# SwiGLU written with tanh, eight PSUM banks assigned by the schedule, and attention spread over the FFN chunks

## The chip, the cores and the metric

The kernel runs on one core of one Trainium2 chip. The metric is the device time of one execution in microseconds (us). A run is called slow where it lies more than 1.5 per cent above the fastest of the same kernel; such runs are left out of every ratio.

In the profile, PE is the tensor engine, PEld its weight loads, DVE the vector engine, ACT the scalar engine, POOL the GpSimd engine, and SP the engine that issues many of the DMAs. All operations are issued through helpers, so a group of instructions is told by its tiles (`psc`, `Hs`), not by its line. A letter at the end of a tile's name is its place in a ring of buffers. The granted clock is the share of its full clock that PE was given; the DMA share adds up packet times over the 16 DMA engines, so it can pass 1.

## The reference

Two stages follow one another: causal attention with a decay bias over 8 batches of 8 heads, 576 positions and head size 64, and then RMS norm and a SwiGLU feed-forward network (FFN) over the resulting 4608 tokens.

```python
scores = scale * np.matmul(q, k.transpose(0, 1, 3, 2))
bias = -(cum[:, :, :, None] - cum[:, :, None, :])      # cum: running sum of max(s, 0)
scores = np.where(causal, -1000000000.0, scores + np.minimum(bias, 0.0))
attn = softmax(scores)                                  # (shortened)
x = np.matmul(attn, v)  # then heads side by side: (4608, 512)   (shortened)
xn = x / rms * rms_g
g = xn @ w_gate                                         # d_ff = 1536
silu = g * (1.0 / (1.0 + np.exp(-g)))
return (silu * (xn @ w_val) @ w_out)
```

## The kernel before

The kernel records its operations in a `Plan`. Each has a duration from a table and a key. A list scheduler then walks through simulated time, takes at each step the ready operation with the lowest key, and so fixes one order for each engine. The chip runs these orders with semaphores; if an operation in the order is late, everything behind it on that engine waits.

The FFN works in nine chunks of 512 tokens. Chunk c needs the attention of the tokens up to 512(c+1), and a batch has 576 tokens, so the attention of batch c+1 runs beside chunk c, and the last two chunks have no attention beside them (the ninth batch doesn't exist). FFN1 is the gate and value products with the gating, FFN2 is the output product.

PSUM is used as four pairs of banks: pairs 0 and 1 serve the scores, pairs 0 to 2 the FFN1 groups, the two halves of pair 2 the outputs in turn, and the two halves of pair 3 everything small.

```python
PS = [pp.tile([128, 2, DM], fp32, name=f"ps{chr(97 + i)}") for i in range(4)]
...  # cut
def small_bank():
    return nxt("small", [PS[3][:, 0, :], PS[3][:, 1, :]])
...  # cut: unit_scores, one pair of heads in one half of the queries
        mms(0.42, items, key=key)
        e = Es[u] = nxt("E", E)
        x = I("act", "activation", 0.93, key=key, kind="exp", out=e, in_=st, func=AF.Exp,
              scale=0.125)
        ...  # cut: causal masks on GpSimd (affine_select)
...  # cut
def ffn1_group(c, o, n, f0, key):
    P = nxt("pair", PS[0:3])
    ...  # cut: eight matmuls for the gate into P[:, 0], for the value into P[:, 1]
    sl = nxt("S", S_sb)
    silu = I("act", "activation", 0.51, key=key, kind="silu", out=sl, in_=P[:, 0, :],
             func=AF.Silu)
    I("dve", "tensor_tensor", 0.61, key=key, out=Hs[:, f0 : f0 + m, o : o + n],
      in0=sl.rearrange("p (i n) -> p i n", i=m),
      in1=P[:, 1, :].rearrange("p (i n) -> p i n", i=m), op=ALU.mult)
    return silu

def ffn2(c, key, step):
    t0 = c * DM
    for tb in range(4):
        O = nxt("O", [PS[2][:, 0, :], PS[2][:, 1, :]])
        ...  # cut: twelve matmuls into O
        o = nxt("osb", osb)
        I("dve", "tensor_copy", 0.61, key=key + step * (tb * FB + FB), out=o, in_=O)
        ...  # cut: o is stored
```

The exponentials and Silu have different tables in ACT. To keep table loads few, the main loop forbids FFN1 of a chunk before the exps of the attention before it, and the exps before all Silus of the chunk:

```python
for c in range(NCH):
    K = 100 * c
    ...  # cut
    new = [ffn1_group(c, o, n, f0, K + 50 * i / len(plan)) for i, (o, n, f0) in enumerate(plan)]
    for x in new:
        R.after(x, *exps)
    silus = new
    b = c + 1
    ...  # cut: preparation of batch b (K and Q transposed, V weighted), loads of batch b + 1
    ffn2(c, K + 50, 0.8)
    if b < B:
        exps = attention(b, K + 40, False)
        for x in exps:
            R.after(x, *silus)
```

So the scores and exps of attention can run beside FFN2 only, which is a third of a chunk's FFN matmuls.

Of the kernel before, what the change touches and what calls it, by code (L numbers as in the profile page):

```python
# [34 lines left out]

class Op:
    __slots__ = ("eng", "us", "lat", "fn", "key", "kind", "preds", "succ", "start", "done",
                 "n", "dma", "name", "wait")


class Plan:
# [4 lines left out]
    TABLE = 1.3  # L46

    def __init__(self):
        self.ops = []
        self.hist = {}  # L50
        self.key = 0.0
        self.last_kind = {}

    def add(self, eng, us, fn, outs, ins, key=None, lat=0.0, kind=None, dma=0.0, name=""):
# [3 lines left out]
        o.preds, o.n = {}, len(self.ops)  # L58
        for aps, write in ((ins, False), (outs, True)):
            for ap in aps:  # L60
                if ap is None or "DRAM" in str(ap.space):
                    continue
                h = self.hist.setdefault(ap.name, ([], []))
                m = _mask(ap)
                for w, wm in h[0]:
                    if wm & m and w is not o:
                        o.preds[w.n] = True
                if write:
                    for r, rm in h[1]:
                        if rm & m and r is not o:  # L70
                            o.preds.setdefault(r.n, False)
                    h[0][:] = [(w, wm & ~m) for w, wm in h[0] if wm & ~m]
                    h[1][:] = [(r, rm & ~m) for r, rm in h[1] if rm & ~m]
                    h[0].append((o, m))
                else:
                    h[1].append((o, m))
# [7 lines left out]
    def schedule(self):  # L84
# [12 lines left out]
        order = []  # L97

# [9 lines left out]

        for o in ops:
            if not left[o.n]:  # L110
                pool.setdefault(o.eng, []).append((ready(o), o))
        while any(pool.values()):
            best = None
            for e, cand in pool.items():
                if not cand:
                    continue
                f = free.get(e, 0.0)
                t = max(f, min(r for r, _ in cand))
                now = [(o.key, o.n, r, o) for r, o in cand if r <= t + 0.02]
                k = min(now, key=lambda x: x[:2])  # L120
# [13 lines left out]
            if o.dma:  # L134
                begin = max(self.dma_free, s + o.us + 1.2)
                self.dma_free = begin + o.dma
                o.done = self.dma_free + 1.4
            order.append(o)
            for q in o.succ:
                left[q.n] -= 1  # L140
                if not left[q.n]:
                    pool.setdefault(q.eng, []).append((ready(q), q))
# [10 lines left out]
def kernel(  # L153
# [35 lines left out]
    NE = 9  # L189
# [19 lines left out]
    ones = pers.tile([BH, S], fp32, name="ones")  # L209
# [3 lines left out]
    peak = pers.tile([128, B, HP], fp32, name="peak")  # L213
    nrm = pers.tile([128, B, 3], fp32, name="nrm")
    knrm = pers.tile([128, 1], fp32, name="knrm")
    mhalf = pers.tile([128, 3], fp32, name="mhalf")
    hones = pers.tile([128, 2], fp32, name="hones")
# [4 lines left out]
    spare = [xnT[0:KP, i, NTOK - H * KC * D : NTOK] for i in range(4)]  # L222
    k_raw, q_raw = (t.rearrange("p (h c d) -> p h c d", h=H, c=KC) for t in spare[0:2])
    k_pk, q_pk = (t.rearrange("p (c h d) -> p c h d", h=H, c=KC) for t in spare[2:4])
# [4 lines left out]
    gB = mp.tile([128, DM], fp32, name="gB")  # L229
# [13 lines left out]
    S_sb = ring(NS, [128, DM], bf16, "S_sb")  # L243
# [3 lines left out]
    PS = [pp.tile([128, 2, DM], fp32, name=f"ps{chr(97 + i)}") for i in range(4)]  # L247

    R = Plan()
# [3 lines left out]
    def I(eng, method, us, key=None, kind=None, dma=0.0, **kw):  # L253
        outs = [kw[n] for n in ("out", "accum_out") if n in kw]
        ins = [a for n, a in kw.items()
               if n not in ("out", "accum_out") and isinstance(a, bass.AP)]
        f = getattr(ENG[eng], method)
        return R.add(eng, us, lambda: f(**kw), outs, ins, key=key, lat=LAT[eng], kind=kind,  # L258
                     dma=dma, name=outs[0].name)
# [5 lines left out]
    def mms(us, items, key=None):  # L265
        def emit():
            for out, lhsT, rhs, st, sp, tr in items:
                if tr:
                    nc.tensor.matmul(out, lhsT=lhsT, rhs=rhs, is_transpose=True, start=st, stop=sp)  # L269
                else:  # L270
                    nc.tensor.matmul(out, lhsT=lhsT, rhs=rhs, start=st, stop=sp)  # L271
        return R.add("pe", us, emit, [i[0] for i in items],
                     [i[1] for i in items] + [i[2] for i in items], key=key, lat=0.22,
                     name=items[0][0].name)
# [7 lines left out]

    def small_bank():
        return nxt("small", [PS[3][:, 0, :], PS[3][:, 1, :]])

    def lay(bank, dt, pattern=None, n=None, **sizes):
        a = bank if dt == fp32 else bank.bitcast(dt)
# [4 lines left out]
    def load_runs(b, which, h0, h1, key):  # L292
        dst, src = ((k_raw, k), (q_raw, q))[which]
        return I("pool", "dma_start", 0.8, key=key, dma=3.95 * (h1 - h0) / 8,
                 out=dst[:, h0:h1, :, :].rearrange("p h c d -> p h (c d)"),
                 in_=src[b, h0:h1, :, :].rearrange("h (p c) d -> p h (c d)", c=KC))
# [22 lines left out]
    def prep_pack(which, h0, h1, key):  # L319
        src, dst = ((k_raw, k_pk), (q_raw, q_pk))[which]  # L320
        I("dve", "tensor_copy", 0.17 * (h1 - h0), key=key, out=dst[:, :, h0:h1, :],
          in_=src[:, h0:h1, :, :].rearrange("p h c d -> p c h d"))

    def prep_transpose(b, which, hp, key, eng):
        src, dst = ((k_pk, KT), (q_pk, QT))[which]
        t = lay(small_bank(), bf16, "p (c t) -> p c t", n=S, c=KC)
        mms(0.4, [(t[:, c, :], src[:, c, 2 * hp : 2 * hp + 2, :].rearrange("p h d -> p (h d)"),
                   ident_bf[0:KP, 0:KP], c == 0, c == KC - 1, True) for c in range(KC)], key=key)
# [4 lines left out]
        else:  # L333
            I("act", "activation", 0.56, key=key, out=o, in_=i, func=AF.Copy)

    def prep_cast(b, which, key):
        src, dst = ((k_nat, k_bf), (q_nat, q_bf))[which]
        out = (KT, QT)[which][b % 2]
        for sc in range(NB):
            n = 128 if sc < 4 else 64  # L340
            I("dve", "tensor_copy", 0.4, key=key, out=dst[0:n, sc], in_=src[0:n, sc])
            I("sp", "dma_start_transpose", 0.7, key=key, dma=0.8,
              out=out[:, :, sc * 128 : sc * 128 + n], in_=dst[0:n, sc])

    def prep_peak(b, hp, key):
        I("dve", "tensor_reduce", 0.68, key=key, out=peak[:, b, hp : hp + 1],
          in_=QT[b % 2][:, hp, :], axis=AX.X, op=ALU.max, apply_absolute_value=True)

    def prep_norm(b, i, key):
        if b < NRUN:  # L350
            n, src = KP, k_pk[:, 2 * i : 2 * i + 2, :, :].rearrange("p c h d -> p (c h d)")
        else:
            n = 128 if i < 2 else 64
            src = k_bf[0:n, 2 * i : min(2 * i + 2, NB), :].rearrange("p c m -> p (c m)")
        w = src.shape[1]
        I("act", "activation", 1.15 if w > DM else 0.74, key=key, out=sq_scr[0:n, 0:w], in_=src,
          func=AF.Square, accum_out=nrm[0:n, b, i : i + 1])
# [18 lines left out]
    def decay(key):  # L376
        I("dve", "tensor_scalar", 0.5, key=key, out=s_all, in0=s_all, scalar1=0.0, scalar2=None,
          op0=ALU.max)
        I("dve", "tensor_tensor_scan", 1.3, key=key, out=cum, data0=ones, data1=s_all, initial=0.0,
# [23 lines left out]
    def check_all(key):  # L403
        I("dve", "tensor_reduce", 0.1, key=key, out=knrm, in_=nrm, axis=AX.XY, op=ALU.max)
        kT = lay(small_bank(), fp32, n=128)[0:1, :]
        mms(0.2, [(kT, knrm, ident_F, True, True, True)], key=key)
        kmax = mp.tile([1, 1], fp32, name="kmax")
        I("dve", "tensor_reduce", 0.2, key=key, out=kmax, in_=kT, axis=AX.X, op=ALU.max)
        qq = mp.tile([128, B, HP], fp32, name="qq")
        I("dve", "tensor_tensor", 0.1, key=key, out=qq, in0=peak, in1=peak, op=ALU.mult)  # L410
        t = lay(small_bank(), fp32, n=2)[0 : BH // 2, :]
        mms(0.1, [(t, qq.rearrange("p b h -> p (b h)"), hones, True, True, False)], key=key)
        qn = mp.tile([BH // 2, 1], fp32, name="qn")
        I("dve", "tensor_reduce", 0.1, key=key, out=qn, in_=t, axis=AX.X, op=ALU.max)
        qT = lay(small_bank(), fp32, n=BH // 2)[0:1, :]
        mms(0.1, [(qT, qn, ident_F[0 : BH // 2, 0 : BH // 2], True, True, True)], key=key)
        ok = mp.tile([1, 4], fp32, name="ok")
        I("dve", "tensor_reduce", 0.1, key=key, out=ok[:, 0:1], in_=qT, axis=AX.X, op=ALU.max)
        I("dve", "tensor_tensor", 0.1, key=key, out=ok[:, 1:2], in0=ok[:, 0:1], in1=kmax,
          op=ALU.mult)  # L420
        I("dve", "tensor_scalar", 0.1, key=key, out=ok[:, 2:3], in0=ok[:, 1:2], scalar1=QK_MAX,
          scalar2=None, op0=ALU.is_le)
        t2 = lay(small_bank(), fp32, n=1)[0:1, :]
        mms(0.1, [(t2, ok1[:, 0:1], ones[:, 0:1], True, True, False)], key=key)
        I("dve", "tensor_tensor", 0.1, key=key, out=ok[:, 3:4], in0=ok[:, 2:3], in1=t2,
          op=ALU.mult)
        I("dve", "tensor_scalar", 0.1, key=key, out=flag, in0=ok[:, 3:4], scalar1=BH - 0.5,
# [6 lines left out]
    def unit_scores(b, u, key, Es, pair):  # L434
        hp, hf = u % HP, u // HP
        st = pair
        items = []
        gs = GROUPS[hf]
        for i, (kb, c0, q0, q1) in enumerate(gs):
            for j in range(2):  # L440
                rs = slice(j * 64, j * 64 + 64)
                items.append((st[:, j, c0 : c0 + q1 - q0],
# [4 lines left out]
        x = I("act", "activation", 0.93, key=key, kind="exp", out=e, in_=st, func=AF.Exp,  # L447
              scale=0.125)
# [3 lines left out]
        if hf == 1:  # L452
            last = e[:, :, 448:512]
            I("pool", "affine_select", 0.27, key=key, out=last, in_=last,
              pattern=[[0, 2], [1, 64]], compare_op=ALU.is_ge, fill=0.0, base=0,
              channel_multiplier=-1)
        return x

    def unit_av(b, u, key, Es):
# [10 lines left out]
        mms(0.04 + 0.06 * len(plan),  # L470
# [4 lines left out]
        I("dve", "reciprocal", 0.17, key=key, out=z, in_=AV[:, :, :, 64])  # L475
        I("dve", "tensor_tensor", 0.35 if hf == 0 else 0.48, key=key,
# [8 lines left out]
    def att_alpha(b, t0, t1, key):  # L485
        m, y = al[b % 2][:, 0, t0:t1], al[b % 2][:, 1, t0:t1]
        I("pool", "tensor_scalar", 0.17, key=key, out=m, in0=ss[b % 2][:, t0:t1],
          scalar1=1.0 / DM, scalar2=1e-6, op0=ALU.mult, op1=ALU.add)
        I("pool", "tensor_tensor", 0.8, key=key, out=y, in0=m, in1=mhalf[:, 0 : t1 - t0],
          op=ALU.pow)  # L490

    def att_scale(b, tb, key):
# [342 lines left out]
```

## Time and profile before

| | before |
|---|---|
| time, median of 3 runs | 430.75 us (430.5 to 431.23) |
| span of the profiled run, mean granted clock | 428.3 us, 0.989 |
| PE busy | 362.4 us, 85% |
| DVE, ACT, POOL busy | 257.2, 205.5, 179.5 us |
| ACT table loads | 16, 20.5 us |
| first FFN1 matmul | 38.6 us |
| end of FFN2 of chunks 0, 6, 8 | 91.2, 350.1, 422.3 us |

The page of the profile, first the busy time of each engine, then PE's busy share in 40 slices (tenths), then the chain of waits that ended last:

```profile
span 428.3 us, 7402 instructions
...
PE 362.4 (85%) x2808; PEld 214.6 (50%) x2843; DVE 257.2 (60%) x498; ACT 205.5 (48%) x327; POOL 179.5 (42%) x267
...
PE   0566978869988998899889988998899989979973
...
PE 76%; DVE 14%; ACT 4%; issue 3%; DMA 2%; POOL 0%; DVEq 0%; ACTq 0%; POOLq 0%
...
```

PE is both the busiest engine and three quarters of the chain. From the list of groups, the table loads (count, then busy us and mean ns of one, then the idle time ahead of them):

```profile
...
L258 ACT ACT_TABLE_LOAD x16 | 20.5, 1283 | 1.1 <-PEq L819 0.8
...
```

A table by stage gives the span of a stretch, then each engine's busy time (and instructions), the clock, the DMA share and GB/s. The four stretches are the start, chunk 0 (with 3.5 us after its end), chunk 4, and chunk 7, which has no new attention beside it:

```profile
...
core 0: us, PE busy (x) PEld busy (x) DVE busy (x) ACT busy (x) POOL busy (x), PEclk, DMA share, GB/s
0.00:38.60 38.60, 15.97 (x173) 11.87 (x174) 23.83 (x57) 16.67 (x27) 26.28 (x45) 1.00 1.07 182
38.60:94.70 56.10, 45.61 (x416) 32.56 (x420) 37.21 (x68) 30.86 (x50) 29.51 (x41) 0.97 0.81 150
224.50:266.40 41.90, 39.02 (x271) 18.63 (x275) 29.38 (x56) 24.10 (x41) 22.48 (x33) 1.00 0.75 134
350.10:386.70 36.60, 33.31 (x159) 15.17 (x160) 13.89 (x22) 8.49 (x14) 0.65 (x1) 1.00 0.08 29
...
```

A steady chunk such as 4 takes 41.9 us and has 39.0 us of PE work; chunk 7 takes 36.6 us with 33.3 us (the busy time of a pipelined matmul record overlaps its neighbours a little; start to start the 144 FFN steps of a chunk take 31.1 us).

Where chunk 7's and 8's gaps come from is seen on the timelines of PE and of DVE at the end. Each line has start, duration, instruction, and in brackets the idle time ahead of it with what ended it:

```profile
...
412.90 2.75 PE L271 MATMUL psc<-wout_sb,Hs 128*128 128x512 bf16 x12 [0.78 <-DVE osbc L258]
416.44 2.75 PE L271 MATMUL psc<-wout_sb,Hs 128*128 128x512 bf16 x11 [0.78 <-DVE osba L258]
...
```

```profile
...
412.16 0.69 DVE L258 COPY osbc<-psc 128x512 f32<-128x512 f32 x1 [2.84 <-PE psc L271]
...
```

The group of matmuls at 412.90 starts just after the copy that began at 412.16 ends (412.85). That copy frees the *other* half of the pair. The two halves alternate, and yet each output waits for the copy of the one just before it: the halves are one tile, and the wait goes by the tile. That costs 0.78 us of idle time for each of the three outputs that follow another (start to start they are 3.54 us apart). Over all nine chunks these waits come to 12.9 us in 22 places (total, times, longest):

```profile
...
PE psc L271 <- DVE osbc L258: 4.6, 7, 0.8
PE psc L271 <- DVE osbb L258: 4.4, 8, 0.8
PE psc L271 <- DVE osba L258: 3.9, 7, 0.8
...
```

### The profile page before, as it was taken

To read this page: it belongs to the slowest core of one execution; us is meant where nothing else is said; L and a number is where in the kernel's file an instruction comes from. 1 tells how busy PE (TensorE), PEld (TensorE's weight loads), DVE (VectorE), ACT (ScalarE), POOL (GpSimd) and SP (SyncE) were. 2 spreads that over 40 slices of the span, in tenths; PEclk is the share of its full clock that TensorE was granted. 3 is DMA by queue.
4 is the path that set the end of the run, shared out by engine and by line. 5 is a ranking of instruction groups with operands and counts; after the bars stand their busy time and mean duration, and the time that the engine had idled before them with its cause. 6 is when DMAs were issued, how large, how long until landed. Compare 5 with 4: busy or idle time off the path is not lost.

```text
span 428.3 us, 7402 instructions
## 1 busy us (share of the span) xinstructions
PE 362.4 (85%) x2808; PEld 214.6 (50%) x2843; DVE 257.2 (60%) x498; ACT 205.5 (48%) x327; POOL 179.5 (42%) x267
## 2 busy tenths in 40 slices
PE   0566978869988998899889988998899989979973
PEld 0444865438844884488444444444443444434421
DVE  4765466895656857766677757765863474314411
ACT  1475326854375537473746375547545842302300
POOL 7666480578445726392629264925300520000000
PEclk9999998999999999999999999999999999999998
DMA  8999994749634995289439951995100010011001
GB/s 116 206 210 206 210 192 68 154 108 215 117 79 106 191 176 98 80 187 182 93 83 207 162 123 51 213 177 105 58 17 0 26 75 1 2 59 40 2 36 67
DMA packets 75673, 48.15 MB, mean 112 GB/s; under 512 B 60144, under 2 KB 66800, under 8 KB 75632
## 3 DMA queue, kind: packets, MB, share of 16 engines
q0 software_dynamic: 12000, 23.60, 29.1%
q1 hardware_dynamic: 63632, 24.02, 28.1%
q8 instruction: 24, 0.39, 0.4%
q14 instruction: 17, 0.14, 0.1%
HBM read 38.16 MB, written 9.44 MB: 111 GB/s over the span
## 4 chain that ended last, share of the span: by engine, by line
PE 76%; DVE 14%; ACT 4%; issue 3%; DMA 2%; POOL 0%; DVEq 0%; ACTq 0%; POOLq 0%
PE psc L271 35%; PE psa L271 17%; PE psb L271 15%; PE psd L271 5%; PE psd L269 3%; DVE x_blka L258 2%; DMA xnT<-in_k_dram 2%; DVE x_blkb L258 2%; DVE Hs L258 2%; DVE xnT L258 1%; DVE osbc L258 1%; ACT S_sbc L258 1%; DVE osbb L258 1%; DVE osba L258 1%; DVE KTa L258 1%
## 5 line engine op out<-in xcount | busy, mean ns | idle before, releaser
L271 PE MATMUL psc<-wout_sb,Hs 128*128 128x512 bf16 x410 | 106.9, 379 | 22.7 <-DVE Hs L258 7.7
L271 PEld LDWEIGHTS <-wg_sb 128*128 128x128 bf16 x624 | 61.4, 100 | 35.4 <-issue 3.4
L271 PEld LDWEIGHTS <-wv_sb 128*128 128x128 bf16 x624 | 61.8, 100 | 34.5 <-issue 2.4
L271 PEld LDWEIGHTS <-Hs 128*128 128x128 bf16 x432 | 37.7, 97 | 61.9 <-issue 29.7
L258 ACT ACTIVATE S_sbb<-psb 128x512 bf16<-128x512 f32 x36 | 21.5, 597 | 53.8 <-PE psb L271 53.8
L258 DVE TENSOR_TENSOR Hs<-S_sbc,psc 128x512 bf16<-128x512 bf16 x36 | 24.7, 687 | 35.8 <-ACT S_sbc L258 25.8
L271 PE MATMUL psa<-xnT,wg_sb 128*128 128x256 bf16 (+1 forms) x205 | 38.6, 323 | 1.6 <-DVE xnT L258 1.4
L258 ACT ACTIVATE S_sbc<-psc 128x512 bf16<-128x512 f32 x36 | 21.5, 597 | 37.7 <-PE psc L271 37.7
L258 DVE TENSOR_TENSOR Hs<-S_sbb,psb 128x512 bf16<-128x512 bf16 x36 | 24.7, 686 | 23.0 <-ACT S_sbb L258 22.6
L271 PE MATMUL psa<-xnT,wv_sb 128*128 128x256 bf16 (+1 forms) x207 | 38.5, 324 | 0.0
L271 PE MATMUL psc<-xnT,wv_sb 128*128 128x256 bf16 (+1 forms) x205 | 37.5, 316 | 1.1 <-ACT S_sbc L258 0.9
L271 PE MATMUL psc<-xnT,wg_sb 128*128 128x256 bf16 (+1 forms) x208 | 38.1, 320 | 0.0
L258 DVE TENSOR_TENSOR Hs<-S_sba,psa 128x512 bf16<-128x512 bf16 x36 | 24.7, 685 | 22.2 <-ACT S_sba L258 22.0
L271 PE MATMUL psb<-xnT,wv_sb 128*128 128x256 bf16 (+1 forms) x207 | 37.1, 313 | 0.5 <-ACT S_sbb L258 0.2
L258 ACT ACTIVATE S_sba<-psa 128x512 bf16<-128x512 f32 x36 | 21.5, 597 | 33.0 <-PE psa L271 31.9
L271 PE MATMUL psb<-xnT,wg_sb 128*128 128x256 bf16 (+1 forms) x203 | 37.0, 316 | 0.2
L258 POOL DMA_DIRECT2D k_nat<-in_k_dram x30 | 25.8, 864 | 6.2 <-DMA xnT<-in_q_dram 2.1
L258 POOL DMA_DIRECT2D q_nat<-in_q_dram x30 | 25.3, 847 | 5.9 <-DMA k_nat<-in_k_dram 3.3
L258 POOL TENSOR_TENSOR vwb<-v_nata,wT 128x512 bf16<-128x512 f32 (+1 forms) x20 | 20.7, 1063 | 16.3 <-DMA v_nata<-in_v_dram 16.3
L269 PE MATMUL psd<-ident_bf,xnT 96*128 96x96 bf16 x96 | 8.2, 244 | 18.6 <-DVE okr L258 10.7
L258 POOL TENSOR_TENSOR vwa<-v_nata,wT 128x512 bf16<-128x512 f32 (+1 forms) x15 | 16.3, 1103 | 17.4 <-DMA v_nata<-in_v_dram 17.4
L258 ACT ACTIVATE sq_scr<-x_blkb 128x512 bf16<-128x512 bf16 x20 | 12.5, 627 | 21.3 <-DVE x_blkb L258 21.0
(160 smaller groups left out, 578.4 us busy)
## 6 DMA issues: line engine op xcount, KB each, us to landing
k_nat<-in_k_dram POOLq DMA_DIRECT2D x24, 256.0 KB, 7.6
q_nat<-in_q_dram POOLq DMA_DIRECT2D x24, 256.0 KB, 10.5
v_nata<-in_v_dram SPq DMA_DIRECT2D x24, 256.0 KB, 8.2
out_dram<-osba SPq DMA_DIRECT2D x12, 256.0 KB, 2.0
out_dram<-osbb SPq DMA_DIRECT2D x12, 256.0 KB, 2.1
out_dram<-osbc SPq DMA_DIRECT2D x12, 256.0 KB, 2.2
v_nata<-in_v_dram POOLq DMA_DIRECT2D x8, 256.0 KB, 13.7
wg_sb<-in_moe_w_gate_dram POOLq DMA_DIRECT2D x2, 768.0 KB, 14.7
```

The source lines that it names most:

```text
L258: return R.add(eng, us, lambda: f(**kw), outs, ins, key=key, lat=LAT[eng], kind=kind, dma=dma, name=outs[0].name)
L269: nc.tensor.matmul(out, lhsT=lhsT, rhs=rhs, is_transpose=True, start=st, stop=sp)
L271: nc.tensor.matmul(out, lhsT=lhsT, rhs=rhs, start=st, stop=sp)
```

## The change

Silu(g) is g(1 + tanh(g/2))/2. Tanh can share a table set with exp, so exps and gates may be mixed freely: the rules in the main loop fall. PSUM becomes eight single banks. The `Plan` assigns a bank when an operation first writes one, with a cap for each group of users. Attention's keys are spread evenly over the chunk. Core of the diff:

```diff
+        def room(o):
+            group, cap, n = o.takes[0].group, o.takes[0].cap, len(o.takes)
+            for t in sorted(f for f, _ in held if f is not None):
+                free = sum(1 for f, _ in held if f is not None and f <= t)
+                busy = sum(1 for f, g in held if g == group and (f is None or f > t))
+                if free >= n and busy + n <= cap:
+                    return t
+            return None
...  (cut)
-    PS = [pp.tile([128, 2, DM], fp32, name=f"ps{chr(97 + i)}") for i in range(4)]
+    banks = [pp.tile([128, DM], fp32, name=f"ps{chr(97 + i)}") for i in range(8)]
...  (cut: ffn1_group)
-        silu = I("act", "activation", 0.51, key=key, kind="silu", out=sl, in_=P[:, 0, :],
-                 func=AF.Silu)
+        G, V = bank("ffn", 6), bank("ffn", 6)
+        I("act", "activation", 0.5, key=key, out=T, in_=G, func=AF.Tanh, scale=0.5)
+        I("dve", "scalar_tensor_tensor", 0.62, key=key, out=u, in0=T, scalar=1.0, in1=G,
+          op0=ALU.add, op1=ALU.mult)
...  (cut: the product with V as before; ffn2)
-            O = nxt("O", [PS[2][:, 0, :], PS[2][:, 1, :]])
+            O = bank("ffn", 6)
-            I("dve", "tensor_copy", 0.61, key=key + step * (tb * FB + FB), out=o, in_=O)
+            I("act", "activation", 0.6, key=key + step * (tb * FB + FB), out=o, in_=O,
+              func=AF.Copy, scale=0.5)
...  (cut: the main loop)
-        for x in new:
-            R.after(x, *exps)
...
-            exps = attention(b, K + 40, False)
-            for x in exps:
-                R.after(x, *silus)
+            attention(b, K + 1, 2.6, 2 if b > 1 else 4)
```

In the cut parts, one exp over a pair of heads becomes two, as the pair of banks is gone. K and Q of batches 0 and 1 are transposed head by head on PE straight from the loaded layout, so that the DVE copies that packed them fall. A DVE search for the largest |Q| (for the check that guards the exponentials) becomes a sum of squares on ACT. The norm's gain moves from a DVE pass of its own into the copy of the transposed tile. The first weights are loaded in pieces, and chunk 0 uses them in that order. The rules that held back the loads of the next batch fall as well. The scheduler also lets DVE, ACT and GpSimd hold back for a more urgent operation that is nearly ready (`AHEAD`), and several durations in its table are new.

## The prediction

> **What bounds the kernel now.** TensorE (PE): 362.4 us busy of 428.3 (85%), 76% of the chain that ended last. A table by stage shows nine FFN chunks after a start of 38.6 us: 56.1, 48.4, 39.4, 42.0, 41.9, 41.9, 41.8, 36.6 us, and 41.6 for the last with the end of the program. From the PE timeline, matmuls issue back to back at 0.432 us per pair of FFN matmuls, so 144 of them cost 31.1 us a chunk. Attention on PE, start to start: 0.33 us for a score unit, 0.32 or 0.65 for an attention-times-V unit, 0.22 for a block of transposes, about 7.6 us a batch. A steady chunk thus has 38.7 us of PE work and takes 41.9. The last two chunks have 31.1 us of work and take about 36: the timeline shows PE waiting 0.8 us for each output copy on VectorE, as only two halves of one PSUM tile serve the output. PE begins at 10.7 us and is about half busy to 38.6; in chunks 0 and 1 attention, packing and FFN run partly one after the other.
>
> **What changes.**
> - Tables: 16 table loads of 1.283 us (by-form groups) fall to about one. The Trainium skill, "ScalarE: Activation LUTs", section "Table sets", puts tanh in the set of exp; the 1283 ns it gives agree with the trace. They are only partly exposed: the point is that attention can now fill FFN1 as well as FFN2.
> - Banks: eight singles instead of four pairs. FFN groups hold up to six, so output copies no longer stop PE.
> - VectorE gets a second pass per group, 108 x 0.69 us = +75 us (estimate from today's 0.687 us product), loses the 36 output copies (25), peak reductions (23.5), packing (8) and most of the 31 us of scaling. Net about 257 to 270 us, some 33 us of a 39 us chunk: near the limit, not at it.
> - ScalarE loses 20.5 us of loads and gains the output copies (36 x 0.6), squares for q (about 20), and split exps (128 x 0.6 against 64 x 1.02): about 240 us.
> - PE work is nearly unchanged; the batch 0 and 1 transposes double in count, perhaps +3 us.
>
> **Sum.** PE starts at about 9 us; about 5 us lost in the start, as chunk 0 may begin on half its tokens; dense work 280 + 61 + 11 = 352; remaining gaps in the seven chunks with attention about 8 (3%); last two chunks 2; end after the last matmul 6 as now. Span 382, time about 384 us.
>
> Predicted 384 us, 8 times in 10 within 375 to 398. Faster by over 2%: 0.97; within 2%: 0.02; slower: 0.01.
>
> **What would show it.** One or two table loads; FFN1 from about 26 us; chunks 1 to 6 with a period of 39 to 40 us and PE over 95% busy; chunks 7 and 8 at 32 each with no wait on output copies; DVE 260 to 275 us, ACT about 240; PE busy about 360.
>
> **What would make it wrong.** VectorE and GpSimd blocking each other (casts take 0.6 to 0.7 us at the mean): gated products come late, the engines' fixed order passes the delay on, period 41 and more. PSUM short where scores and small tiles leave four banks to the FFN. Weights late, since the gate, value and second-batch loads share one queue at some 206 GB/s: PE would wait in chunk 0, and the time would be near 395.

## The result, and the profile after

The changed kernel is correct and takes 396.07 us (median of 4 runs, 395.82 to 396.64), against 430.62 us for the kernel before on the same chip (4 runs, 429.82 to 431.23). The ratio is 0.920, 95% interval 0.918 to 0.922. All ratios here are the mean time of one kernel's fast runs over that of the other's of the same rounds, so not quite the ratio of the medians. The time is inside the predicted range and 12 us above the predicted 384.

The page after, the same lines:

```profile
span 394.2 us, 7505 instructions
...
PE 354.7 (90%) x2746; PEld 192.3 (49%) x2746; DVE 263.5 (67%) x521; ACT 228.6 (58%) x460; POOL 180.0 (46%) x275
...
PE   3669935959999979999999999999999999999993
...
PE 72%; DMA 9%; DVE 8%; POOL 7%; issue 2%; ACT 1%; DVEq 0%; POOLq 0%; ACTq 0%
...
```

PE is busy 90% of a span of 394.2 us. There is one table load (1.3 us) where there were 16. The 40 slices show where PE isn't full: apart from the last slice, all of it lies in the first fifteen (9.86 us each, so up to 148 us). From there on every slice reads 9.

The chunks ended (last FFN2 matmul) as follows, in us. The differences are each chunk's period.

| | 0 | 1 | 2 | 3 | 4 | 5 | 6 | 7 | 8 |
|---|---|---|---|---|---|---|---|---|---|
| before | 91.2 | 139.4 | 182.5 | 224.5 | 266.4 | 308.2 | 350.1 | 386.7 | 422.3 |
| after | 92.8 | 130.2 | 173.6 | 211.5 | 249.3 | 287.2 | 325.0 | 356.5 | 387.6 |

Chunk 0 ends 1.6 us later than before although FFN1 begins at 30.1 us instead of 38.6. Chunks 1 to 6 take 232.2 us instead of 258.9 (26.7 less), the last two 62.6 instead of 72.2 (9.6 less). These sum to 34.7 us; with 0.6 us more after the last matmul that is the span's 34.1 us.

A table by stage, cut at the point where PE's idle time ends (columns as before: span, then PE, PEld, DVE, ACT and POOL busy, clock, DMA share, GB/s):

```profile
...
5.40:90.00 84.60, 60.05 (x692) 43.60 (x692) 54.59 (x107) 51.91 (x107) 63.08 (x95) 0.92 1.04 185
90.00:143.20 53.20, 50.25 (x440) 32.41 (x439) 40.38 (x76) 35.58 (x74) 33.73 (x46) 0.98 1.11 193
143.20:356.50 213.30, 213.30 (x1473) 102.26 (x1472) 148.66 (x306) 129.71 (x265) 79.05 (x126) 0.99 0.51 94
356.50:394.20 37.70, 31.11 (x145) 13.88 (x142) 16.50 (x24) 10.15 (x17) 0.00 (x0) 0.96 0.10 37
...
```

From 143.2 to 356.5 us the records of PE fill the stretch without a gap: 213.30 of 213.30. The whole span is then 5.4 us to the first matmul, 24.6 + 3.0 = 27.5 us idle before 143 us, 354.7 us busy, and 6.6 us after the last matmul.

The output copies no longer stop PE. In the last chunk the groups start 2.59 us apart, each in a bank of its own:

```profile
...
379.68 2.75 PE L349 MATMUL psa<-wout_sb,Hs 128*128 128x512 bf16 x12
382.27 2.75 PE L349 MATMUL psb<-wout_sb,Hs 128*128 128x512 bf16 x12
...
```

The largest waits of PE (total, times, longest):

```profile
...
PE psd L349 <- POOL Ea L332: 13.6, 2, 10.5
...
PE psh L347 <- DVE x_blkb L332: 2.8, 1, 2.8
PE psh L349 <- DVE u_sbc L332: 2.5, 1, 2.5
...
```

The longest, 10.5 us, is in chunk 0. On PE:

```profile
...
52.35 1.05 PE L349 MATMUL psc<-xnT,wv_sb 128*128 128x256 bf16 x8
63.94 0.51 PE L349 MATMUL psd<-vwb,Ea 128*128 128x65 bf16 x6 [10.54 <-POOL Ea L332]
...
64.85 1.90 PE L349 MATMUL psg<-xnT,wg_sb 128*128 128x256 bf16 x8
...
70.13 1.03 PE L349 MATMUL pse<-xnT,wg_sb 128*128 128x256 bf16 x8
71.00 1.04 PE L349 MATMUL psa<-xnT,wv_sb 128*128 128x256 bf16 x8
...
```

PE waits for `Ea`, the first causal mask of batch 1, which GpSimd does at 63.25. GpSimd's own timeline:

```profile
...
49.26 0.88 POOL L332 DMA_DIRECT2D q_nat<-in_q_dram  x1 [2.38 <-DMA wout_sb<-in_moe_w_out_dram]
53.14 0.88 POOL L332 DMA_DIRECT2D q_nat<-in_q_dram  x1 [2.99 <-DMA wout_sb<-in_moe_w_out_dram]
...
57.56 0.69 POOL L332 DMA_DIRECT2D q_nat<-in_q_dram  x1 [2.32 <-DMA k_nat<-in_k_dram]
58.27 5.03 POOL L332 TENSOR_TENSOR vwb<-v_nata,wT 128x512 bf16<-128x512 f32 x5
63.25 0.63 POOL L332 TENSOR_SCALAR_AFFINE_SELECT Ea<-Ea 128x512 bf16<-128x512 bf16 x1
...
```

Ahead of the mask in GpSimd's fixed order stand the loads of batch 2's K and Q. They are needed only for the attention beside chunk 1, but each issue of a load waits for an earlier load to land, 2.4, 3.0 and 2.3 us here; where the trace names a load as what ended the wait, it is the eighth load before it in GpSimd's own order. The operands in the packed trace show why: GpSimd's loads signal eight semaphores in turn (99 to 106), and an issue waits for the semaphore that it will signal itself; the issue at 49.26 waits for 103, which the load of `wout_sb` completed at 48.98. So this limit is in the program as it was built; no run shows one of the DMA queue itself. The schedule's cost table knows no such limit. It expected these issues to be over early, put them ahead of the masks, and the weighting of V (5.03 us) behind them.

The matmuls at 64.85 right after the wait start 1.70 us before the next group, where the same group takes 0.87 us at 70.13 (71.00 − 70.13). The Trainium skill, "TensorE: Matmul & The Clock Gate", section "What's actually happening", says that the clock falls to half after at least one idle window of about 3.4 us; the factor of two here agrees, and the granted clock is 0.50 from 56.7 to 66.9 us. But PE need not be idle for all of such a window: the clock was 0.50 also from 87.4 to 90.8 and from 142.0 to 145.4 us, after waits of only 2.83 and 2.50 us (in the 3.4 us before, PE was busy 0.83 and 1.05 us). A long wait thus costs more than its own length.

A second kind of wait comes at 83 us. The DVE and GpSimd timelines side by side:

```profile
...
83.33 4.60 DVE L332 TENSOR_SCALAR x_blkb<-x_blkb,alb 128x512 bf16<-128x512 bf16 x2
...
```

```profile
...
83.90 1.05 POOL L332 TENSOR_TENSOR vwa<-v_nata,wT 128x512 bf16<-128x512 f32 x1
...
85.83 1.05 POOL L332 TENSOR_TENSOR vwa<-v_nata,wT 128x512 bf16<-128x512 f32 x1
...
87.75 3.25 POOL L332 TENSOR_TENSOR vwa<-v_nata,wT 128x512 bf16<-128x512 f32 x3
...
```

Two scalings of `x_blkb`, of which the median takes 0.353 us, take 4.60 us, while GpSimd is weighting V. PE waits 2.83 and 1.21 us for them at 86 and 88 us.

### The profile page after: what moved, and what is told of

The parts are those of the page before. It is cut to its first block, busy times and chain, and to the rows that moved or that the text cites. A ratio compares the mean times of both kernels' runs of the same rounds, so it can differ in the third digit from the quotient of the medians.

```text
span 394.2 us, 7505 instructions
## 1 busy us (share of the span) xinstructions
PE 354.7 (90%) x2746; PEld 192.3 (49%) x2746; DVE 263.5 (67%) x521; ACT 228.6 (58%) x460; POOL 180.0 (46%) x275
## 4 chain that ended last, share of the span: by engine, by line
PE 72%; DMA 9%; DVE 8%; POOL 7%; issue 2%; ACT 1%; DVEq 0%; POOLq 0%; ACTq 0%
PE psb L349 11%; PE psd L349 10%; PE psa L349 10%; PE psg L349 9%; PE psc L349 9%; PE pse L349 8%; PE psh L349 8%; PE psf L349 7%; DMA k_nat<-in_k_dram 4%; DMA xnT<-in_q_dram 3%; DMA v_nata<-in_v_dram 2%; DVE x_blkb L332 2%; DVE k_bf L332 2%; POOL xnT L332 1%; POOL vwb L332 1%
## 5 line engine op out<-in xcount | busy, mean ns | idle before, releaser
L349 PE MATMUL psb<-wout_sb,Hs 128*128 128x512 bf16 x108 | 26.2, 388 | 0.0
L349 PE MATMUL pse<-xnT,wg_sb 128*128 128x512 bf16 (+1 forms) x92 | 19.4, 345 | 1.9 <-DVE xnT L332 1.9
L349 PE MATMUL psg<-xnT,wv_sb 128*128 128x512 bf16 (+1 forms) x84 | 18.5, 349 | 0.0
L349 PE MATMUL psc<-xnT,wv_sb 128*128 128x512 bf16 (+1 forms) x84 | 17.9, 343 | 0.0
L349 PE MATMUL psd<-wout_sb,Hs 128*128 128x512 bf16 x72 | 17.6, 386 | 0.0
L349 PE MATMUL psf<-xnT,wg_sb 128*128 128x512 bf16 (+1 forms) x80 | 16.5, 337 | 0.1
L332 ACT ACTIVATE sq_scr<-k_bf 128x1024 bf16<-128x1024 bf16 (+1 forms) x18 | 16.4, 909 | 0.3
L332 ACT ACTIVATE sq_scr<-q_bf 128x1024 bf16<-128x1024 bf16 (+1 forms) x18 | 16.3, 908 | 0.2
L332 DVE CAST k_bf<-k_nat 128x512 bf16<-128x512 f32 (+1 forms) x30 | 16.4, 571 | 0.0
L332 DVE CAST q_bf<-q_nat 128x512 bf16<-128x512 f32 (+1 forms) x30 | 15.9, 543 | 0.0
```

The lines of the kernel that those rows point to most:

```text
L332: o = R.add(eng, us, lambda: f(**{n: real(a) for n, a in kw.items()}), outs, ins, key=key, lat=LAT[eng], kind=kind, dma=dma, name=outs[0]. ...
L349: nc.tensor.matmul(out, lhsT=lhsT, rhs=rhs, start=st, stop=sp)
```

## The experiments

All kernels gave correct results. Groups were run with the kernel before in the same rounds: the first four (430.8 us), the next four (430.56), the next three (430.62) and the last (430.59). The changed kernel itself is compared through its ratio of 0.920 to the kernel before. Any edit to operations or keys reshuffles the whole schedule, since the scheduler is greedy; a few microseconds may come from that alone. e8 below gains 5.7 us without a cause that was found, so a gain of that size in the total is no proof by itself; the waits and the ends of chunks count for more.

### The wait at 53 us: loads ahead of masks

**e1_late.** Is it the order on GpSimd that makes PE wait? The loads of batch 2's K and Q are made to follow the first four masks of batch 1.

```diff
             attention(b, K + 1, 2.6, 2 if b > 1 else 4)
+            if b == 1:
+                for o in lq:      # the loads of K and Q of batch 2
+                    o.wants = [m.n for m in R.ops[n0:] if m.eng == "pool"][0:4]
```

> The changed kernel, but the ten K and Q loads of batch 2 may be issued by GpSimd only after the first four masks of batch 1 (before: ahead of them). Theory A (the ORDER of GpSimd's instructions: each load issue waits until the eighth load before it has landed, and the masks and the scaling of V stand behind ten such issues): the wait of 10.5 us of TensorE for the mask of batch 1 at 53.4 us falls under 3 us, time 383 to 390 us (396.1 now). Rival B (the DATA are late: V of batch 1 lands late [...]): V was already landed by about 46 us by issue time plus landing time, so if B holds the wait shrinks by under 3 us and the time stays above 392.

Measured: 392.7 us (391.45 to 395.03), ratio 0.9127 (0.9051 to 0.9203). The 10.5 us wait is gone; chunk 0 ends at 77.9 us instead of 92.8. But chunk 2 ends at 171.4 us instead of 173.6. On PE in this run:

```profile
...
102.89 0.37 PE L351 MATMUL psa<-QTa,KTa 64*128 64x256 bf16 x1 [4.64 <-DMA QTa<-q_bf]
...
```

```profile
...
130.13 0.61 PE L349 MATMUL psg<-ident_bf,x_blka 128*128 128x128 bf16 x4 [6.38 <-DVE x_blka L334]
...
```

So the order did make that wait, as the first theory said, but of the 15 us won by chunk 0 only 2 were left two chunks later: PE waited for the transposed Q of batch 2 and for the scaling of its output instead. The time misses the 383 to 390 us of the first theory and lies where the rival put it, above 392; it is the wait that decides between them. The gain of the whole, some 3 us, isn't sure by the interval.

**e2_ring.** Instead of moving loads by hand, the scheduler is told of the limit: a load on GpSimd can't start before the eighth load before it has landed.

```diff
                 for r, o in cand:
+                    if e == "pool" and o.dma and len(self.landed) >= 8:
+                        r = max(r, self.landed[-8])
...
+                if e == "pool":
+                    self.landed.append(o.done)
```

> The changed kernel, with one line more in its scheduler: a GpSimd load is not ready before the eighth load before it has landed; it then puts masks and V scaling ahead of blocked loads by itself. Theory A: both mask waits go (3.1 us at 17.7 us, for batch 0, under 1.5; 10.5 us at 53.4 us under 3), and with them the half-speed matmuls just after them; time 379 to 387 us. Rival B (late data): 390 or more.

Measured: 387.4 us (385.94 to 388.97), ratio 0.8991 (0.8922 to 0.9061): 0.4 us above the 379 to 387 that the theory expected, and below the rival's 390. Chunks 0 to 2 end at 78.0, 115.3 and 167.3 us. The wait at 53 us has shrunk from 10.5 us to 0.6, and one long wait is left:

```profile
...
124.23 0.61 PE L352 MATMUL psf<-ident_bf,x_blka 128*128 128x128 bf16 x4 [5.99 <-DVE x_blka L337]
...
```

In that stretch DVE first waited 3.6 us for the norm's factor, and then its three scalings took 3.22 us beside GpSimd's weighting of V.

A missing rule in the cost model thus explains about 9 us (0.9200 − 0.8991 = 0.021 of 430). The order found this way seems to keep more of the gain than the hand-made one, though their intervals overlap.

**e5_ring_halves.** A plan in halves (256 tokens at a time) lets FFN1 of a chunk start when the first half of its tokens is there. The changed kernel uses it for chunk 1; here, with e2's scheduler, chunks 2 and 3 have it too, as they had in the kernel before.

```diff
-        plan = first if c == 0 else halves if c == 1 else whole
+        plan = first if c == 0 else halves if c < 4 else whole
```

> The version whose scheduler knows of the eight loads (387.4 us), and FFN1 of chunks 2 and 3 split in halves of 256 tokens too, as chunk 1 is. Theory: its remaining 6.0 us wait (PE for the scaled output of batch 2 at 124 us) is there as chunk 2 starts only when three blocks of batch 2 are done; with halves one block is enough. The wait falls under 2 us and the time to 378 to 384 us. Rival (the loads of batch 2 set the pace and the wait only moves): 385 us or more, with the waits of PE at another place between 90 and 150 us.

Measured: 386.73 us (385.78 to 390.55), ratio 0.8977 (0.8937 to 0.9016): no gain over e2 that the runs could show. Chunk 2 ends at 168.7 us. The 6.0 us wait became one of 3.55 us (at 164 us) and several of about 1 us. The work of batch 2 is late; how the chunk that waits for it is cut changes nothing, as the rival said.

### What the parts of the change are worth

**e3_before_tanh.** The kernel before with tanh alone: same table set, output copies on ACT, but the pairs of banks and the order rules kept.

```diff
-        silu = I("act", "activation", 0.51, key=key, kind="silu", out=sl, in_=P[:, 0, :],
-                 func=AF.Silu)
+        silu = I("act", "activation", 0.51, key=key, out=sl, in_=P[:, 0, :],
+                 func=AF.Tanh, scale=0.5)
+        I("dve", "scalar_tensor_tensor", 0.62, key=key, out=sl, in0=sl, scalar=1.0,
+          in1=P[:, 0, :], op0=ALU.add, op1=ALU.mult)
```

> The kernel before, with the tanh form of the gate alone (bf16 tanh, output copies on ScalarE with the factor one half), its banks and its rule 'all exps, then all gates' kept. Theory A (the tables cost little by themselves; they matter because they force the rule): 16 table loads become 1, the time stays within 2% of before: 420 to 434 us; chunks 3 to 6 stay at 41 to 42.5 us each. Rival C (the 20 us of table loads were most of the gain): 412 us or less.

Measured: 439.32 us (439.06 to 439.8), ratio 1.021 (1.0138 to 1.0282). It is not faster but about 2% slower, so neither expectation held. The table loads did fall to one. DVE rose from 257.2 to 300.2 us, for the second pass came on top of the packing, peak and scaling passes that the full change removes. A steady chunk took 42.6 to 44.7 us.

**e4_before_tanh_norule.** The same without the rules on the order.

```diff
-        for x in new:
-            R.after(x, *exps)
...
-            for x in exps:
-                R.after(x, *silus)
```

> As the run with tanh alone, and the rule 'all exps, then all gates' is dropped too; still four PSUM pairs, attention still placed at the second half of the chunk by its keys. Theory A (the gain needs the rule gone, banks to let both run, and keys that spread attention): a small gain, 412 to 428 us. Rival C': the rule was all of it, and the time falls to 405 or less.

Measured: 438.12 us (434.93 to 439.33), ratio 1.0191 (1.0115 to 1.0266). Again neither. The output copies, now on ACT, still stop PE:

```profile
...
383.52 2.75 PE L271 MATMUL psc<-wout_sb,Hs 128*128 128x512 bf16 x12 [0.73 <-ACT osbc L258]
387.00 2.32 PE L271 MATMUL psc<-wout_sb,Hs 128*128 128x512 bf16 x10 [0.73 <-ACT osba L258]
...
```

With pairs of banks, then, a common table set and the freedom to mix were worth nothing in this kernel. I had expected 3 to 18 us from them. e4 differs from e3 in the rules alone, so it is the freedom to mix that gained nothing with these keys. e3 changes tables, output copies and DVE's load together; what the tables alone are worth isn't shown.

**e6_silu_back.** The reverse: the changed kernel with Silu back, everything else kept.

```diff
-        I("act", "activation", 0.5, key=key, out=T, in_=G, func=AF.Tanh, scale=0.5)
-        I("dve", "scalar_tensor_tensor", 0.62, key=key, out=u, in0=T, scalar=1.0, in1=G,
-          op0=ALU.add, op1=ALU.mult)
+        I("act", "activation", 0.51, key=key, kind="silu", out=u, in_=G, func=AF.Silu)
```

> The changed kernel with the gate by Silu again (one VectorE pass per group instead of two), banks and spread of attention kept; the built program then has some 112 table loads that run. Theory (spreading needs one table set): 144 us of loads on ScalarE, which becomes a limit beside PE: time 410 to 450 us, steady chunks 42 us or more. Rival (tanh is dispensable, the banks and the spread do it): under 402 us.

Measured: 488.65 us (484.92 to 489.78), ratio 1.1343 (1.1269 to 1.1417), outside the expected 410 to 450. The profile has 112 table loads, 143.7 us. In 60 us of a chunk (191.6 to 251.6 us) ACT is busy 51.2 us and PE 42.6. On ACT:

```profile
...
259.04 1.28 ACT L332 ACT_TABLE_LOAD   x1
260.34 0.60 ACT L332 ACTIVATE u_sba<-pse 128x512 bf16<-128x512 f32 x1
260.95 1.28 ACT L332 ACT_TABLE_LOAD   x1
...
```

Exps and Silus alternate, each with a load ahead of it: 1.28 + 0.60 us, and the next pair begins 1.91 us later. With this scheduler and these keys, spread attention thus needs the common table set, though e3 and e4, which have that set without the spread, gain nothing. The Trainium skill, "ScalarE: Activation LUTs", section "What ACT_TABLE_LOAD costs", gives 1283 ns for a load, which agrees, and about 1380 ns for a drain besides, of which this timeline shows nothing.

**e7_bunched.** The changed kernel with attention's keys put together behind FFN1 instead of spread.

```diff
-            attention(b, K + 1, 2.6, 2 if b > 1 else 4)
+            attention(b, K + STEP * 96, 0.1, 2 if b > 1 else 4)
```

> The changed kernel, attention of each batch keyed together at the start of FFN2 instead of spread over the chunk. Theory (the even spread is what makes the steady chunks gapless): chunks 3 to 6 go from 37.1 to 38.0 us up to 39 to 42, time 402 to 416 us. Rival (the banks alone do it; order in the chunk hardly matters): steady chunks within 0.7 us of now, time within 392 to 401 us.

Measured: 404.14 us (401.98 to 405.27), ratio 0.938 (0.9328 to 0.9433), as expected. From 165.5 to 333.3 us four chunks average 41.95 us, which is the period of before, but they are not alike: 46.3, 36.4, 47.1 and 38.0 us. The two long ones hold a wait of 4.45 us (at 170 us) and one of 5.31 us (at 255 us), each with 6.8 us at half the clock. So the spread is worth 16.4 us in chunks 3 to 6 (167.8 against 151.4). Net it is about 8 us (0.938 − 0.920 = 0.018 of 430), because chunk 2 here ends 8.1 us earlier than in the changed kernel: the mask wait in chunk 0 was only 2.97 us.

**e8_out_two_banks.** Is it the number of banks that freed the outputs? Outputs get two banks of their own at a time, FFN1 four, instead of six shared.

```diff
-        G, V = bank("ffn", 6), bank("ffn", 6)
+        G, V = bank("ffn", 4), bank("ffn", 4)
...
-            O = bank("ffn", 6)
+            O = bank("out", 2)
```

> The changed kernel, output tiles of FFN2 limited to two banks of their own and FFN1 to four, as the pairs of before had it for outputs. Theory (free banks hide the output copies): PE waits about 0.5 to 0.8 us at each output tile where nothing else fills in, surely in the last two chunks (8 tiles, +3 to 6 us) and in part in the others: time 400 to 415 us. Rival (banks matter little with the spread): within 394 to 399 us.

Measured: 390.38 us (389.66 to 391.95), ratio 0.9068 (0.9028 to 0.9108). It is faster than the changed kernel; both expectations missed. The end:

```profile
...
376.38 2.75 PE L349 MATMUL psa<-wout_sb,Hs 128*128 128x512 bf16 x12
378.97 2.54 PE L349 MATMUL psg<-wout_sb,Hs 128*128 128x512 bf16 x11
...
```

The last two chunks take 31.5 and 31.1 us as before this edit, and no output waits. The cap of two is one of the plan only: the banks themselves still rotate (`psf`, `psa`, `psg`, `psb` in the last chunk). What it shows is that a plan with two outputs at a time suffices; six are not needed. Why it is 5 to 6 us faster isn't settled. The mask wait is still there (10.3 us), but the waits for `x_blkb` and `u_sbc` after 80 us are not; a different order that happens to miss GpSimd is as good an explanation as any.

### DVE and GpSimd

**e9_v_on_dve.** If the long scalings come from GpSimd's weighting of V at the same time, they must vanish when DVE does the weighting itself.

```diff
             for sc in range(NB):
-                prep_v(b, sc, "pool", K - 8 + sc)
+                prep_v(b, sc, "dve", K - 8 + sc)
```

> The changed kernel, with V of batches 1 to 7 scaled by VectorE instead of GpSimd (35 tiles of about 1.05 us leave GpSimd, 35 of about 0.65 us come to VectorE). Theory D (VectorE's bf16 scalings and casts are held up whole by GpSimd's back-to-back multiplies: a cast of 0.42 us at the median took 3.85 once, a scaling of 0.35 us took 2.57): the longest cast and the longest scaling fall under 1.5 us, and PE's waits on x_blkb (4.9 us) and u_sbc (2.5) fall to under 2 in sum; time 386 to 393 us although VectorE is busier by some 20 us. Rival (the long ones come from DMA writes or reads of those tiles): they stay above 2.5 us. The 10.5 us wait for the mask of batch 1 shrinks too, by up to 5 us, as the masks no longer stand behind 5 us of V scaling.

Measured: 388.08 us (fast runs 387.33 to 389.98; a fourth run was slow), ratio 0.9026 (0.8976 to 0.9077), as expected. The longest cast on DVE fell from 3.85 us to 0.85, the longest scaling from 2.57 us to 0.80, though DVE had more to do. The casts of K (shortest, median and longest in ns), in the changed kernel and here:

```profile
...
L332 DVE CAST k_bf<-k_nat x30: 404/418/3850, 74.1 to 249.2; 128x512 bf16<-128x512 f32 x24, 64x512 bf16<-64x512 f32 x6
...
```

```profile
...
L332 DVE CAST k_bf<-k_nat x30: 406/419/782, 74.2 to 241.9; 128x512 bf16<-128x512 f32 x24, 64x512 bf16<-64x512 f32 x6
...
```

The mask wait stays (8.7 us). So the long instructions did come from GpSimd's work beside them. The Trainium skill, "SBUF — State Buffer", section "Who interferes with whom", says so: casts, copies and scalings with a scalar in certain modes share ports with GpSimd, and whichever comes second blocks until the first is done. In one point the trace differs: in the changed kernel the cast at 137.3 us took 3.85 us, to 141.2, while GpSimd ran not one but four instructions one after the other, from 137.3 to 140.9. DVE did not get its turn in between.

**e10_ring_scale_on_act.** With e2's scheduler, the scaling moves from DVE to ACT, which that section says never waits. Where ACT does it, in e11, the trace agrees: all forty scalings took 0.70 to 0.72 us.

```diff
-        I("dve", "tensor_scalar", 0.25, key=key, out=x, in0=x,
-          scalar1=al[b % 2][:, 1, tb : tb + 1], scalar2=None, op0=ALU.mult)
+        I("act", "activation", 0.55, key=key, out=x, in_=x, func=AF.Copy,
+          scale=al[b % 2][:, 1, tb : tb + 1])
```

> The version whose scheduler knows of the eight loads (387.4 us), with the scaling of the attention output by ScalarE instead of VectorE. Theory D: ScalarE is not held up by GpSimd, the 6.0 us wait at 124 us loses the 2.3 us that three scalings took too long, and the smaller waits of 0.9 to 1.1 us at 75 us go: time 381 to 386 us. Rival (the early chunks are paced by the loads, and any wait taken away comes back elsewhere before 170 us, as with the halves): 386 to 389 us, end of chunk 2 still between 166 and 169 us.

Measured: inconclusive. Three of four runs were slow (395.14 to 399.3 us); the one fast run took 389.28 us.

**e11_ring_both.** e2's scheduler, e9's weighting on DVE and e10's scaling on ACT together.

> The eight-load scheduler, V scaled by VectorE and the output scaled by ScalarE. Theory: both mask waits and the hold-ups of VectorE are gone: 374 to 383 us, end of chunk 2 before 163 us. Rival (loads set the pace of chunks 1 and 2): 384 us or more, end of chunk 2 at 166 us or later, with the 16 DMA queues busy throughout 60 to 150 us as in the other runs.

Measured: 385.86 us (fast runs 384.58 to 386.16; a fourth was slow), ratio 0.895 (0.8908 to 0.8992). Only 1 to 2 us better than e2, which the intervals don't make sure; the rival's 384 or more holds, but its other mark, chunk 2 at 166 us or later, isn't reached. Chunks 0 to 2 end at 75.9, 111.2 and 164.3 us, so chunk 2 takes 53 us. On SP, which issues the DMA transposes of K and Q of batch 2:

```profile
...
83.38 6.56 SPq L337 DMA_TRANSPOSE QTa<-q_bf  x1
...
90.90 5.70 SPq L337 DMA_TRANSPOSE QTa<-q_bf  x4
...
```

The casts they need were done at 79.2 us, but the last of these five transposes is issued only at 96.6 us, and the scores of batch 2 begin at 99.6. Much of this is SP's own time: the first of the five was 6.56 us in issue, where the run's median for Q is 1.70. In this stretch the DMA share is 1.1 to 1.3 all along. A transpose of K or Q took 2.4 to 2.7 us from issue to landing in the kernel before (medians of the four tiles over all batches); 4.6 to 6.7 us in the changed kernel; 4.7 to 10.7 us here.

### The start without the transposes of batch 2

**e12_batch2_by_runs.** Batch 2 is prepared as batches 0 and 1 are: loaded as bf16 and transposed on PE, with no DMA transposes. This is added to e11. The sums of squares of batches 0 and 2 get earlier keys, since the buffers are used again.

```diff
-    NRUN = 2
+    NRUN = 3
...
-                 out=spare[2 * b + which][:, h0:h1, :, :].rearrange("p h c d -> p h (c d)"),
+                 out=spare[(2 * b + which) % 4][:, h0:h1, :, :].rearrange("p h c d -> p h (c d)"),
```

> The eight-load scheduler, V scaled by VectorE, output scaled by ScalarE (386.0 us), and K and Q of batch 2 loaded like those of batches 0 and 1: cast to bf16 by the DMA in runs of six tokens and transposed by TensorE, instead of fp32 rows of one head, a VectorE cast and ten DMA transposes. This halves the bytes written for it (2.36 to 1.18 MB) and takes ten DMA transposes away from 80 to 97 us, when the DMA engines are full; it adds about 3 us of PE work. Theory (DMA sets the pace of chunks 1 and 2: the transposes of Q of batch 2 were issued over 83 to 97 us though the casts were done at 79): chunk 2 ends at 150 to 158 us instead of 164, time 373 to 381 us. Rival (latency of the attention chain or VectorE sets it): chunk 2 ends at 162 us or later, time 384 us or more.

Measured: 379.39 us (fast runs 377.6 to 380.03; a sixth was slow), ratio 0.8793 (0.8747 to 0.8839), a time as expected. Chunks 0 to 2 end at 78.0, 120.6 and 158.4 us (150 to 158 had been expected for chunk 2), and PE has no wait worth naming after 87 us. The stages before 143 us:

```profile
...
5.40:90.00 84.60, 74.07 (x887) 53.51 (x889) 61.31 (x119) 68.49 (x136) 56.43 (x89) 1.00 1.20 206
90.00:143.20 53.20, 52.11 (x456) 31.40 (x459) 45.73 (x90) 40.75 (x84) 26.17 (x42) 1.00 1.12 179
...
```

PE was busy 126.2 us up to 143.2 us, against 60.05 + 50.25 = 110.3 in the changed kernel. The difference, 15.9 us, is the whole difference of the spans (394.2 − 378.3). Part of the gain over e11 is the clock: there PE had half of it from 115.1 to 128.8 us, here nowhere before the last matmul (mean 0.995 against 0.979). This is the best version: 12% faster than the kernel before, some 4% faster than the changed one. Which property of the edit helped is left open: fewer bytes on the queues, fewer transposes, or the order on SP. The transposes that remain are still slow (medians 6.7 to 9.9 us), but no wait of PE for them shows.

## Why the prediction was right or wrong

**Direction and mechanism: right.** One table load came in place of 16. Chunks 7 and 8 took 31.5 and 31.1 us (predicted 32) with no wait on output copies. DVE was busy 263.5 us (predicted 260 to 275), ACT 228.6 (about 240), PE 354.7 (about 360). From 143 us on PE has no gap, so the spread works as the prediction said; e7 shows that it is the spread, and e6 that with this scheduler it needs the common table.

**The sum, term by term.**

| term of the sum | predicted | measured |
|---|---|---|
| before the first matmul | 9 | 5.4 |
| PE idle after that (5 + 8 + 2) | 15 | 27.5 |
| PE work | 352 | 354.7 |
| after the last matmul | 6 | 6.6 |
| span | 382 | 394.2 |

**The step that failed** is "about 5 us lost in the start, as chunk 0 may begin on half its tokens", with "remaining gaps in the seven chunks with attention about 8 (3%)". I took the loss to be spread over all chunks and small. In fact none of it lies after 143 us, and before that it is 27.5 us. FFN1 began at 30.1 us instead of "about 26", and chunk 0 ended later than in the kernel before. The runs show three causes in a row; the third came to light only when the first was taken away:

- GpSimd's loads wait for the eighth load before them, by the program's eight semaphores, and the schedule didn't know: 10.5 us of wait at 53 us. e1 and e2 remove it. e2 gains about 9 us.
- DVE is held while GpSimd weights V: casts and scalings of up to 3.85 us, waits of 2.8, 1.2 and 2.5 us on PE. e9 removes the long instructions and gains about 7 us (0.920 − 0.9026 = 0.017 of 430), but e11 shows that this doesn't add to e2's gain.
- K and Q of batch 2 come late (seen in e1 and e11): SP issues their DMA transposes late, and over the run these take two to four times as long to land as in the kernel before. e12, without them, gains what e11 could not; whether by the transposes' own time, the bytes or the order on SP is not separated.

**What was named as a risk.** "VectorE and GpSimd blocking each other" happened, but not with the effect that was named (period 41 and more): the steady period was 37.8 us. "Weights late, since the gate, value and second-batch loads share one queue" came nearest: the time was to be near 395, and it was 396. That agreement is luck, as it wasn't the weights that PE waited for. It was the masks behind the loads on the engine that issues them.

**Two sizes were off in the other direction.** I took the period of chunks 1 to 6 to be 39 to 40 us; the steady one is 37.8. Attention on PE is then 37.8 − 31.1 = 6.7 us of a chunk, not 7.6. One part is seen on the timeline: an attention-times-V unit of 12 matmuls, for which I took up to 0.65 us from the kernel before, takes 0.36 us start to start in the steady chunks. This concealed part of the loss at the start: of the 354.7 us that PE was busy, FFN (280) and attention (8 x 6.7 = 54) leave about 21 for the rest, some of it at half the clock, where the sum had 11 (an estimate from these numbers). That the two nearly cancel is luck.

**Where I was wrong about the cause of the gain.** The prediction says of the table loads that "the point is that attention can now fill FFN1 as well as FFN2". e3 and e4 show that this permission by itself gained nothing (1.02 with or without the rules). e7 gives 0.938 without the spread, so most of the gain from 1.02 to 0.938 belongs to what lies between e4 and e7: single banks, the DVE work taken away, the start and the other changes of keys. One part can be assigned: between its first and last matmul PE was idle 49 us before and 27.5 after, and 12.9 us of what went were the waits for output copies that share a tile, none of which is left. In the last two chunks they make about 5.7 of the 9.6 us (six times 3.54 − 2.59). The rest isn't separated.

## What to carry to other kernels

Before a fixed order is trusted, look for what its cost model doesn't know: here eight semaphores that loads share in turn, an engine that is held while its neighbour works, and transposes that took longer in a busier schedule. All three struck only in the first third, where the DMA queues were full, and a prediction from steady chunks didn't see them. When a wait is removed and little time is gained, look for the next wait on the same path before calling the theory false: e1's 15 us in chunk 0 came back two chunks later, and it took e12 to keep them.

## What the Trainium skill lacked or had wrong

- No page has it: a program built as this one gives GpSimd's loads eight semaphores in turn, so that each issue waits until the eighth load before it has landed. In the changed kernel such issues waited up to 3.0 us each, and a mask behind them made PE wait 10.5 us. It is a limit of the program; none of the chip is shown.
- "DMA: Bandwidth & Descriptors", section "DMA Transpose (X-bar)": nothing on how long a transpose takes to land among other DMAs. The medians here were 2.4 to 2.7 us in the kernel before and 4.6 to 6.7 us in the changed one, up to 10.7 us in e11; that the load is the reason isn't shown.
- "ScalarE: Activation LUTs", section "What ACT_TABLE_LOAD costs": 1283 ns for the load agrees. The drain of about 1380 ns for every switch is not to be seen: in e6 a load and an activation of 0.60 us repeat every 1.91 us.
- "SBUF — State Buffer", section "Who interferes with whom": "Whoever issues first gets the shared pair for the whole instruction" leaves out that the engine in waiting may not get its turn when several instructions of the other follow each other. One cast (median 0.42 us) took 3.85 us beside four GpSimd instructions in a row.
